# Two slots of attention scores at a time in shared PSUM banks, and rows turned by DMA instead of by TensorE

## The chip, the cores and the metric

The kernel runs on one core of a Trainium2 chip. The metric is the device time of one execution in microseconds; three runs of the kernel before gave 2230.16, 2236.23 and 2237.89, so the time before is 2236.23 (their median).

A core has five engines with queues of their own: TensorE (PE, with its weight loads shown as PEld), VectorE (DVE), ScalarE (ACT), GpSimd (POOL) and SyncE (SP, which issues nearly all DMAs here). TensorE writes to PSUM, eight banks of 512 float32 columns on each of 128 partitions; DVE and ACT read it from there.

## The reference

Four layers in a row, each added to its input after a layer norm: a Fourier mixing layer, an attention layer, and the same two again. S = 2048 rows, D = 640 columns.

```python
a = jnp.einsum("bsd,ed->bse", x, dft_hid_re)
b = jnp.einsum("bsd,ed->bse", x, dft_hid_im)
y = jnp.einsum("ts,bse->bte", dft_seq_re, a) - jnp.einsum("ts,bse->bte", dft_seq_im, b)
...
B, S, D = x.shape
H = 32; Dh = D // H; W = 256
qkv = (x @ wqkv).reshape(B, S, 3, H, Dh)   # -> q, k, v
scores = jnp.einsum("bhqd,bhkd->bhqk", q, k) * (Dh ** -0.5)
mask = (idx[:, None] - idx[None, :] >= 0) & (idx[:, None] - idx[None, :] < W)
p = _softmax(jnp.where(mask[None, None], scores, -1e9), axis=-1)
return o.transpose(0, 2, 1, 3).reshape(B, S, D) @ wo
```

The attention has 32 heads of 20 columns and looks back over a window of 256 rows.

## The kernel before, in words

Precision first: a float32 operand is split into a high and a low float16 part, and a product is three float16 products (high x high, high x low, low x high). So a projection over 640 columns is 5 x 3 = 15 matmuls into one PSUM bank.

The program is spectral(0), attention(0), spectral(1), attention(1). The attention handles 16 row tiles of 128 rows in 8 blocks of two tiles (256 rows). Its step is a *slot* g: one row tile and one pair of heads, 256 slots in all; 32 slots make a block, and four slots (both tiles, two head pairs) a *quad* n.

For each slot, in the order in which TensorE gets it:

- `scores(g)`: queries x keys, 128 rows by up to 384 keys for each of the two heads, into the tile `sp` (two banks). The keys have 62 rows in the array; the two heads lie in its two halves, at rows 0 and 64. DVE masks the diagonal block (`copy_predicated`, L1058) and takes the largest of each row (`tensor_reduce`, L1062). Every fourth slot `part_tops` splits the row maxima into float16 parts.
- `by_key(g - 7)`: the same scores keys x queries, with the row maximum as an extra row, into the tile `tp` (two other banks). ACT turns them into probabilities (L1106) in SBUF (`ptq`), and POOL clears what the mask forbids (`affine_select`, L1111 and L1113).
- For a quad: `hand_on` turns the maxima by four transposes and ACT copies them into the stacked queries (`copy_tops`, L1083, two copies); `values` multiplies probabilities by values into the bank `pv` (32 float32 matmuls) and ACT takes it to SBUF (L1139); `back` turns that by two transposes into the same bank, and DVE divides by the sum of the row (L1154, L1155).

Between these stands the *fill*: the projections of the next block (`proj_qk`, 10 units of 15 matmuls of 256 columns; `proj_v`, 4 units of 15 of 320), the output projection of finished tiles (`out_tile`, two units of 15 of 320 a tile), and in the first attention the first products of the next spectral layer (kind "next"). A planner written in Python gives the fill out in time: `run_fill(ns)` runs single matmuls until a budget is used, between 400 ns and what is due, times a factor by the slot's place in the quad (`FILL`). All instructions of TensorE are tied to this order (`issue_after`).

Row tiles must be turned (columns to partitions) before a projection: `turned` makes five transposes on TensorE for each float16 part into a bank of its own (`p3`), and ACT or DVE copies it to SBUF (L958, L956). It serves the normed rows of a block (`rows_turn`), attention outputs (`out_turn`) and rows for the next spectral layer (`next_turn`, stored to DRAM already turned and fetched by `Hidden.fetch`). These are fill units of the kind "turn".

The eight banks in an attention: `sp` two, `tp` two, `pv` one, `p3` one (turns and handing on), `pf` two in rotation (all fill).

DVE also runs the layer norms of coming rows in small pieces (`slow_step`, one a slot), behind the row maximum of the slot.

Of the kernel before, what the change touches and what calls it, by code (L numbers as in the profile page):

```python
# [34 lines left out]
FILL = (1.3, 1.12, 0.28, 1.3)  # L35
# [4 lines left out]
OUT_STEPS = (4, 2, 8)  # L40
LAST_STEPS = (1, 258)
LAST_FROM = 3
HAND_LAG = 4
KEY_LAG = 7
VALUE_LAG = 13
BACK_LAG = 15
# [4 lines left out]
NORM_STEPS = (4, 9)  # L51
# [10 lines left out]
def body(ctx: ExitStack, tc: tile.TileContext, x_in, cmat, whid, wqkv, wo, out):  # L62
# [140 lines left out]
    class Hidden:  # L203
# [18 lines left out]
        def fetch(self, s):  # L222
            load(self.xt(s).rearrange("p a b c -> p (a b c)"), self.xt_src[s])
# [121 lines left out]
    def spectral(layer, res_src, hidden, first):  # L345
        with ExitStack() as st:
# [170 lines left out]
            def main_a(r, j):  # L517
                res = [keep.tile([P, D], F32, tag="res", name="res", bufs=4) for k in range(2)]
# [173 lines left out]
            else:  # L692
                side.append(hidden.rest)
# [75 lines left out]
    def attention(layer, proj, dst, final):  # L769
        with ExitStack() as st:  # L770
# [7 lines left out]
            if layer == 0:  # L778
                ps = banks("ps")
                pv_ = banks("pv")  # L780
            else:
                pv_ = banks("pv")
                ps = banks("ps")
            p3 = banks("p3")

            def new_turn():

                return p3.tile([P, 512], F32, tag="f", name="pt") if in_turn[0] else new_f()

            in_turn[0] = True  # L790
            VS_ = {}
            pv = None
# [38 lines left out]
            def out_turn(i, k):  # L831
                if k:
                    X2[i] = keep.tile([P, D], F32, tag="res", name="x3", bufs=4)
                    load(X2[i], x2_d[i])
                else:
                    OT[i] = sb.tile([P, 2, ND, P], F16, tag="ot", name="ot", bufs=2)
                yield from turned(OS[i // 2][:, :, i % 2], k, OT[i])
                done.add((i, k))

            def last_out(i, d0, d1):  # L840

                if d0 == 0:
                    x3 = keep.tile([P, D], F32, tag="res", name="x3", bufs=4)
                    load(x3, x2_d[i])
                    OT[i] = (sb.tile([P, 2, ND, P], F16, tag="ot", name="ot", bufs=2),
                             ps.tile([P, 2, 512], F32, tag="ts"[i % 2 == 0], name="acc"), x3)
                ot, acc, x3 = OT[i]
                for k in range(2):
                    yield from turned(OS[i // 2][:, :, i % 2], k, ot, d0, d1)
                for n in range(2):  # L850
                    yield from out_products(ot, acc[:, n], n, d0, d1)
                if d1 < ND:
                    return
                for n in range(2):
                    cs = slice(n * 320, (n + 1) * 320)
                    nc.vector.scalar_tensor_tensor(x3[:, cs], acc[:, n, :320], beta, x3[:, cs], op0=OP.mult, op1=OP.add)
# [13 lines left out]
            def out_tile(i):  # L870
                ot = OT[i]
                x3 = x2 = X2.pop(i)
                for n in range(2):
# [10 lines left out]
                    if n == 0:  # L884
                        yield 136
                done.add((i, 2))
                if final:
                    load(dst[i], x3)
# [3 lines left out]
            slow, live = deque(), deque()  # L892

            def new_xs():

                while len(live) > 1:
                    for g in live.popleft():
                        for _ in g:
                            pass
                live.append([])  # L900
                return keep.tile([P, 2, D], F16, tag="xs", name="xs", bufs=2)
# [6 lines left out]
            def next_norm(i, x3):  # L908
                ys = []
                yield from norm_steps([x3], ys)  # L910
                xs = new_xs()
                split(xs[:, 0], xs[:, 1], ys[0], nc.gpsimd)
                xt = keep.tile([P, 2, ND, P], F16, tag="xto", name="xto", bufs=2)
                live[-1].extend(next_turn(i, xs, xt, k) for k in range(2))
                if i < NT - 2:
                    fill.extend(Unit(now[0] + TURN_STEPS, g, "turn", now[0], [], True) for g in live[-1])

            def split_wo():

                fs = [keep.tile([P, D], F32, tag="res", name="wst", bufs=4) for n in range(2)]  # L920
# [3 lines left out]
                for n in range(ND):  # L924
# [3 lines left out]
                    if n + 2 < ND:  # L928
                        fs.append(keep.tile([P, D], F32, tag="res", name="wst", bufs=4))
# [3 lines left out]
            def rows_norm(b, x2s):  # L933
# [3 lines left out]
                for t, y in enumerate(ys):  # L937
                    xs = new_xs()
                    split(xs[:, 0], xs[:, 1], y, nc.gpsimd)
                    live[-1].extend(rows_turn(b, xs, t, k) for k in range(2))  # L940
                    fill.extend(Unit(now[0] + ROW_STEPS, g, ("rows", b), now[0], [], True) for g in live[-1])
                    yield

            def rows_turn(b, xs, t, k):
                yield from turned(xs, k, proj.rows[b][0][:, t])
                done.add(("rows", b, t, k))

            def turned(xs, k, o, d0=0, d1=ND):
                pt = new_turn()
# [11 lines left out]
            def next_turn(i, xs, xt, k):  # L961
                yield from turned(xs, k, xt)
                if k:
                    load(xu_d[i], xt.rearrange("p a b c -> p (a b c)"))

            OS, OT, X2, done = {}, {}, {}, set()
            lastd = [0]
# [5 lines left out]
            class Unit:  # L973


                def __init__(self, at, gen, kind, due, need=(), turn=False, ns=0):
                    self.at, self.gen, self.kind, self.due, self.need, self.turn = at, gen, kind, due, need, turn
                    self.ns, self.n = ns, 0

                def ready(self):  # L980
                    return self.at <= now[0] and all(k in done for k in self.need)
# [3 lines left out]
            def next_unit(turn=None):  # L985
# [322 lines left out]
```

## Time and profile before

| | |
|---|---|
| runs | 2230.16, 2236.23, 2237.89 us |
| profiled execution | span 2233.0 us; a time of its own beside the span isn't given |
| first attention, first to last score product | about 590 to 1135 us |
| second attention, likewise | about 1685 to 2202 us |
| TensorE busy, whole span | 95% |

The page lists for each engine the busy time and its share. "Busy" of TensorE counts a pipelined matmul to its modelled end, so two matmuls that start 109 ns apart are each shown as about 273 ns long, and their overlap is counted once. The chain of waits follows the last instruction back to what released each step; a row is start, length and what ran. In groups of instructions stand count, busy time, mean ns of one, and the idle time of the engine just before them with what ended it.

### The profile page before, as it was taken

The numbers are of one execution on the slowest core, as the hardware profiler recorded it, in microseconds if no ns is written. First come the engines' busy times: TensorE is split into PE (matmuls) and PEld (weight loads), VectorE is DVE, ScalarE is ACT, GpSimd is POOL, SyncE is SP. The second block draws the span as 40 slices with busy tenths as digits, with TensorE's granted clock in tenths as the row PEclk, the third lists the DMA queues.
The fourth block names the chain that finished last, engine by engine and source line by source line (L and its number), as shares of the span: only waits on it lengthen the run. The fifth ranks groups of instructions, "written<-read, shape, count | busy, mean of one in ns | idle before, by whom it ended". The sixth has DMA issues, their size and how long they took to land.

```text
span 2233.0 us, 55112 instructions
## 1 busy us (share of the span) xinstructions
PE 2122.0 (95%) x21985; PEld 1494.7 (67%) x21985; DVE 1646.4 (74%) x3577; ACT 1288.8 (58%) x2155; POOL 1391.6 (62%) x1788
## 2 busy tenths in 40 slices
PE   7999899899999999999899999999998999999998
PEld 4767566676666766677566777777675666677765
DVE  8887958767677887887858758585767777777664
ACT  5434455443467777777754443434434777777775
POOL 5775968758355665566446858586674555566443
PEclk9999999999999999999999999999999999999999
DMA  6664646455533422333424536364743323332231
GB/s 252 219 224 143 229 138 225 156 188 175 142 79 67 103 71 73 94 91 84 134 79 160 193 127 212 110 207 145 256 133 96 83 63 85 93 87 59 57 80 37
DMA packets 187607, 292.96 MB, mean 131 GB/s; under 512 B 13908, under 2 KB 120660, under 8 KB 178004
## 3 DMA queue, kind: packets, MB, share of 16 engines
q1 hardware_dynamic: 186772, 288.77, 42.1%
q8 instruction: 172, 2.82, 0.5%
q14 instruction: 87, 0.71, 0.1%
q10 hardware_dynamic: 576, 0.66, 0.1%
HBM read 202.51 MB, written 86.87 MB: 130 GB/s over the span
## 4 chain that ended last, share of the span: by engine, by line
PE 59%; DVE 12%; DMA 4%; issue 3%; POOL 2%; ACT 2%; SPq 1%; DVEq 0%; POOLq 0%; ACTq 0%
PE pf L115 24%; PE pv L115 8%; PE y L115 7%; PE sp L115 5%; PE x L115 5%; PE z L115 5%; PE tp L115 3%; DVE m L1062 3%; DVE sp L1058 2%; PE pt L115 2%; DVE cc L489 1%; DMA res<-accd 1%; DMA x2d<-res 1%; PE acc L115 1%; DMA qs<-qkd 1%
## 5 line engine op out<-in xcount | busy, mean ns | idle before, releaser
L115 PEld LDWEIGHTS <-cc 128*128 128x128 f16 x5376 | 525.1, 98 | 215.6 <-issue 10.6
L1106 ACT ACTIVATE ptq<-tp,shift,alpha 128x768 f32<-128x768 f32 (+2 forms) x512 | 486.2, 950 | 163.6 <-PE tp L115 155.6
L115 PEld LDWEIGHTS <-big 128*128 128x128 f16 x4320 | 408.5, 98 | 151.9 <-issue 40.5
L1062 DVE TENSOR_REDUCE m<-sp 128x2 f32<-128x512 f32 (+1 forms) x512 | 345.1, 674 | 16.8
L1058 DVE COPY_PREDICATED sp<-mask,sp 128x256 f32<-128x256 int32 x448 | 190.8, 426 | 188.2 <-PE sp L115 176.5
L115 PE MATMUL pf<-early,big 128*128 128x256 f16 x2400 | 313.9, 274 | 2.9 <-ACT early L401 2.5
L1111 POOL TENSOR_SCALAR_AFFINE_SELECT ptq<-ptq 128x512 f32<-128x512 f32 x224 | 145.5, 649 | 265.4 <-ACT ptq L1106 261.7
L486 ACT ACTIVATE cc<-cs 128x512 f16<-128x512 f32 x256 | 151.6, 623 | 254.6 <-POOL cs L478 124.1
L115 PE MATMUL y<-zc,cc 128*128 128x320 f16 x1728 | 263.8, 300 | 2.4 <-DVE pf L512 2.4
L115 PE MATMUL pf<-big 128*128 128x320 f16 x1680 | 245.6, 304 | 19.2 <-DVE zc L257 9.3
L489 DVE SCALAR_TENSOR_TENSOR cc<-cs,cc 128x512 f16<-128x512 f32 x256 | 255.2, 1012 | 9.9 <-ACT cc L486 9.7
L489 DVE SCALAR_TENSOR_TENSOR cc<-cq,cc 128x512 f16<-128x512 f32 x192 | 198.7, 1036 | 0.0
L1113 POOL TENSOR_SCALAR_AFFINE_SELECT ptq<-ptq 128x512 f32<-128x512 f32 x256 | 163.9, 640 | 43.1 <-ACT ptq L1106 43.1
L115 PE MATMUL pv<-ptq,v 128*32 128x128 f32 (+1 forms) x3840 | 183.7, 330 | 0.0
L115 PE MATMUL z<-zc,cc 128*128 128x320 f16 x1152 | 178.5, 299 | 2.0 <-ACT cc L486 1.0
L115 PE MATMUL x<-zc,cc 128*128 128x320 f16 x1152 | 179.7, 299 | 0.0
L115 PE MATMUL sp<-ks,qs 62*128 62x256 f16 (+1 forms) x1792 | 153.6, 248 | 20.8 <-DVE m L1062 18.6
L115 PE MATMUL pf<-big,early 128*128 128x320 f16 x960 | 162.3, 301 | 6.4 <-DVE x L883 6.4
L1083 ACT ACTIVATE qs<-pt 2x512 f16<-2x512 f16 x224 | 131.0, 585 | 42.7 <-PE pt L115 40.0
L115 PE MATMUL tp<-qs,ks 62*128 62x128 f16 x2688 | 150.1, 217 | 3.2 <-ACT ptq L1106 2.7
L115 PE MATMUL pf<-bo,ot 128*128 128x320 f16 x840 | 147.2, 302 | 3.3 <-DVE ot L956 2.8
L167 POOL TENSOR_TENSOR xs<-lny,xs 128x640 f16<-128x640 f32 x63 | 94.2, 1497 | 83.3 <-ACT xs L166 82.6
(144 smaller groups left out, 3525.3 us busy)
## 6 DMA issues: line engine op xcount, KB each, us to landing
cq<-in_cmat_dram SPq DMA_DIRECT2D x64, 1024.0 KB
accd<-res SPq DMA_DIRECT2D x96, 320.0 KB
res<-accd SPq DMA_DIRECT2D x96, 320.0 KB
x<-x2d SPq DMA_DIRECT2D x64, 320.0 KB
qkd<-early SPq DMA_DIRECT2D x160, 128.0 KB
ks<-qkd SPq DMA_DIRECT2D x108, 160.0 KB
qs<-qkd SPq DMA_DIRECT2D x84, 160.0 KB
x2d<-res SPq DMA_DIRECT2D x32, 320.0 KB
```

Source lines behind the costliest of these rows:

```text
L115: i = getattr(nc.tensor, what)(*args, **kw)
L167: eng.tensor_tensor(lo, y, hi, op=OP.subtract)
L486: nc.scalar.activation(cc[m][:, 0], f, AF.Copy, scale=C_UP)
L489: nc.vector.scalar_tensor_tensor(cc[m][:, 1], f, C_UP, cc[m][:, 0], op0=OP.mult, op1=OP.subtract)
L1058: nc.vector.copy_predicated(sp[:, :, 2 * P:3 * P], mask[:, None, :].to_broadcast([P, 2, P]), far)
L1062: topped[0] = nc.vector.tensor_reduce(TOP[g // 4][:, g % 4], sp[:, :, c0:3 * P], axis=AX.X, op=OP.max).ins
L1083: nc.scalar.activation(o, handed[n][rs].rearrange("r (i p) t -> r i p t", i=2), AF.Copy)
L1106: nc.scalar.activation(q[:, h:h + 2, a0 + first:a0 + 3], tp[:, :, first * P:3 * P].rearrange("p a (b c) -> p a b c", c=P), AF.Sigmoid, bia ...
L1111: nc.gpsimd.affine_select(out=q[:, :, a0], in_=q[:, :, a0], pattern=[[0, 4], [-1, P]], base=0, channel_multiplier=1, compare_op=OP.is_gt, ...
L1113: ins = nc.gpsimd.affine_select(out=q[:, :, a0 + 2], in_=q[:, :, a0 + 2], pattern=[[0, 4], [1, P]], base=0, channel_multiplier=-1, compare ...
```

## The change

1. The planner's step is two slots, G = 0 to 127: both head pairs of the half quad at once. The lags are set anew in these steps.
2. Scores and keyed scores no longer have four separate banks. Two tiles of three banks (`st`, one for each half of the head pair) hold the scores of two slots in their first 768 columns and the keyed scores of two slots in the other 768. So the middle bank of each holds both. A block of the second slot that crosses a bank's edge is cut into two matmuls. DVE's and ACT's instructions keep their number and size but each takes one half (`pi`) of two slots instead of two halves of one, and in a step they are called in the order: ACT half 1, DVE half 0, DVE half 1, ACT half 0.
3. `pv` and `p3` are gone; values, back, handing on and fill share the two banks of `pf` in rotation.
4. The fill runs in whole units of 15 matmuls, one a step (a second one in even steps if there is enough budget). `hand_on` comes after the unit, at once followed by both copies.
5. Rows are turned by transposing DMAs on SP (`turn_load`), SBUF to SBUF for normed rows and attention outputs; rows for the next spectral layer are stored as they are and turned by the fetch. A turned tile counts as ready eight slots after its issue (`TURN_LAG`). Only the last two output tiles of each attention are still turned on TensorE. What was left to turn at the start of the second spectral layer (`hidden.rest`) goes away.
6. Buffers: attention outputs have three (`os`) instead of two, the four `res` buffers become two and two, and outputs are due 40 slots later.

The core of the diff:

```diff
-FILL = (1.3, 1.12, 0.28, 1.3)
+SECOND = 1500
+FULL_TO = 244
-OUT_STEPS = (4, 2, 8)
+OUT_STEPS = (4, 40, 8)
-HAND_LAG = 4
-KEY_LAG = 7
-VALUE_LAG = 13
-BACK_LAG = 15
+HAND_LAG = 1
+KEY_LAG = 3
+VALUE_LAG = 5
+BACK_LAG = 6
+TURN_LAG = 8
+UNIT = 384
...
+    def turn_load(out, in_):
+
+        with ExitStack() as order:
+            if in_turn[0] and loads:
+                order.enter_context(tc.issue_after(loads[-1]))
+            i = nc.sync.dma_start(out.rearrange("p a b c -> p (a b) c"), in_, transpose=True)
+        loads.append(i.ins)
...
         def fetch(self, s):
-            load(self.xt(s).rearrange("p a b c -> p (a b c)"), self.xt_src[s])
+            turn_load(self.xt(s), self.xt_src[s])
...
+            st = [ps.tile([P, 4 * UNIT], F32, name=f"st{k}") for k in range(2)]
+            sps, tps = ([t[:, k * 2 * UNIT:(k + 1) * 2 * UNIT].rearrange("p (e c) -> p e c", e=2) for t in st] for k in range(2))
...
-            def rows_turn(b, xs, t, k):
-                yield from turned(xs, k, proj.rows[b][0][:, t])
-                done.add(("rows", b, t, k))
+            def rows_turn(b, xs, t):
+                turn_load(proj.rows[b][0][:, t], xs.rearrange("p a b -> p (a b)"))
+                done["rows", b, t] = now[0] + TURN_LAG
...
+                for e in range(2):
...
+                        at = UNIT * e
+                        cuts = [c for c in (c0, 512 - at, c1) if c0 <= c <= c1]
+                        for d0, d1 in zip(cuts, cuts[1:]):
+                            for pi in range(2):
+                                if d1 > d0:
+                                    r = slice(64 * pi, 64 * pi + 3 * DH + 2)
+                                    matmul(st[pi][:, at + d0:at + d1], qs[r, p0 + e, t0:t0 + P],
+                                           KS[kb][r, p0 + e, k0 + d0 - c0:k0 + d1 - c0], start=True, stop=True)
...
+            def largest(G, pi):
...
+                nc.vector.copy_predicated(sp[:, :, 2 * P:3 * P], mask[:, None, :].to_broadcast([P, 2, P]), far)
+                topped[0] = nc.vector.tensor_reduce(TOP[n][:, 2 * k:2 * k + 2, pi], sp[:, :, c0:3 * P], axis=AX.X, op=OP.max).ins
...
+            def hand(n):
+                hand_on(n)
+                for pi in range(2):
+                    copy_tops(n, pi)
...
+            for G in range(NS // 2 + 1):
+                now[0] = g = 2 * G
...
+                    scores(G)
+                keyed = 0 <= G - KEY_LAG < NG // 2
+                if keyed:
+                    by_key(G - KEY_LAG)
+                if keyed:
+                    probabilities(G - KEY_LAG, 1)
+                if g < NG:
+                    for pi in range(2):
+                        largest(G, pi)
+                    if G % 2:
+                        part_tops(G // 2)
+                if keyed:
+                    probabilities(G - KEY_LAG, 0)
+                n = due(G, BACK_LAG)
+                if n is not None:
+                    back(n)
...
+                credit[0] += 2 * max(rate, 400)
+                filled = run_unit()
+                if filled and credit[0] > SECOND and G % 2 == 0:
+                    run_unit()
+                n = due(G, HAND_LAG)
+                if n is not None:
+                    if filled:
+                        hand(n)
+                    else:
+                        kept = n
```

More of the change, by code (lines that the diff above doesn't have):

```diff
@@ L50 @@
 TURN_STEPS = 8
-NORM_STEPS = (4, 9)
+NORM_STEPS = (4, 10)
 ROW_STEPS = 3
@@ L517, in main_a @@
             def main_a(r, j):
-                res = [keep.tile([P, D], F32, tag="res", name="res", bufs=4) for k in range(2)]
+                res = [keep.tile([P, D], F32, tag=f"res{j % 2}", name="res", bufs=2) for k in range(2)]
                 for k in range(2):
@@ L959, in turned @@
                 yield 56
[L961 to L967, printed above, removed]
+            OS, OT, X2, done = {}, {}, {}, {}
+            lastd, outs = [0], []
             credit = [0.0]
@@ L1022, in flush @@
             def flush(kind):
-                for u in sorted((u for u in fill if u.kind == kind and u.turn), key=lambda u: u.due):
-                    fill.remove(u)
-                    while step(u):
-                        pass
                 while any(u.kind == kind for u in fill) or (unit[0] and unit[0].kind == kind):
```

303 lines of the change are left out of this document (137 added, 166 removed).

## The prediction

> **What bounds the kernel now.** I read the page first, then a table of stretches cut at the first and last score product of each attention, then the chain of waits inside the second attention, then the engines' lists of instructions around it.
>
> ```profile
> span 2233.0 us, 55112 instructions
> PE 2122.0 (95%) x21985; PEld 1494.7 (67%) x21985; DVE 1646.4 (74%) x3577; ACT 1288.8 (58%) x2155; POOL 1391.6 (62%) x1788
> ```
> ```profile
> 590.00:1135.00 545.00, 517.92 (x6905) 360.28 (x6904) 437.30 (x1132) 406.13 (x614) 301.94 (x550) 0.99 0.34 89
> 1135.00:1176.00 41.00, 36.48 (x360) 23.03 (x356) 17.52 (x54) 19.58 (x36) 19.68 (x29) 0.96 0.30 103
> 1685.00:2202.00 517.00, 497.94 (x6721) 345.62 (x6720) 386.71 (x953) 382.92 (x575) 280.61 (x534) 1.00 0.30 73
> 2202.00:2233.00 31.00, 23.16 (x261) 14.18 (x259) 8.17 (x25) 12.48 (x20) 9.22 (x18) 1.00 0.16 54
> ```
>
> Columns: stretch, us, then busy time of PE, PEld, DVE, ACT, POOL, clock, DMA share, GB/s. The attentions (545 and 517 us, tails 41 and 31) are the only stages the change touches but for 40 turns that open the second spectral layer. TensorE is idle for 27 and 19 us of the two; it bounds them, in order. DVE is next with 80% and 75%.
>
> ```profile
> 2044.86 0.27 PE sp L115 x4
> 2045.13 0.17 PE tp L115 x6
> 2045.30 1.42 PE pf L115 x12
> 2046.72 0.22 PE pt L115 x4
> ...
> 2047.38 1.44 PE pv L115 x32
> ...
> 2050.56 0.28 PE pt L115 x5
> ...
> 2051.82 0.37 PE pv L115 x2
> 2052.19 1.64 PE pf L115 x15
> 2053.83 0.27 PE sp L115 x4
> ```
> ```profile
> 1135.76 2.04 PE pf L115 x15
> ```
>
> Chain of waits, start and length: four slots of the second attention, with nothing but TensorE on the chain; the last line is a unit of 320 columns in the first attention. One slot costs sp 0.27 + tp 0.17 and 0.10 more when the array goes back to full height (twelve pf products of 0.109 would be 1.31, not 1.42; the two transposes of pv likewise 0.27 and 0.10). In 0.27 some 0.10 is the way in: inside a slot sp takes 0.17, as in the tp line. So 0.54 a slot, 0.20 of it switching. A quad's values take 1.44, its back 0.27, its handing on 0.22, five row turns 0.28, a unit 1.64 (query, key) or 2.04 (value, output).
>
> Check on the second attention: 64 quads x (4 x 0.54 + 0.22) = 152, 60 x (1.44 + 0.27) = 103, 70 x 1.64 = 115, about 55 units x 2.04 = 113, 260 turns x 0.056 = 15, idle 19: 517, as measured. The prices hold.
>
> **The change part by part.**
>
> (1) Two slots at a time: one way in and out for two slots, 0.10 + 2 x 0.17 + 2 x 0.17 + 0.10 = 0.88, and about 0.02 for the block that is cut at a bank's edge in every other step: 0.90 instead of 1.08. 128 steps x 0.18 = 23 us a layer, **-46**.
>
> (2) Row turns off TensorE.
>
> ```profile
> L115 PE MATMUL pf<-early,big 128*128 128x256 f16 x1050 | 139.2, 273 | 0.0
> L115 PE MATMUL pt<-idh,xs 128*128 128x128 f16 x240 | 21.3, 219 | 0.0
> L115 PE MATMUL pt<-idh,os 128*128 128x128 f16 x140 | 12.4, 219 | 0.0
> L115 PE MATMUL pt<-idh,os 128*128 128x128 f16 x140 | 12.4, 219 | 0.0
> L115 PE MATMUL pt<-idh,xs 128*128 128x128 f16 x120 | 10.6, 219 | 0.0
> ```
>
> Groups of TensorE (busy, mean ns | idle): three of the first attention, two of the second. 380 + 260 turns x 0.056 (five in 0.28) = 36, and 40 of the next layer's first turns, 2: **-38**. Their PSUM copies on ACT and DVE go too; those engines were not the bound, so nothing more.
>
> (3) The old waits. The 27 and 19 us of idle belong to the old order (the largest: sp on DVE, below). I take all off, **-46**, and charge the new order's own waits.
>
> ```profile
> PE sp L115 <- DVE m L1062: 16.8, 30, 1.1
> PE sp L115 <- DVE m L1062: 11.4, 26, 0.9
> ```
>
> (4) The new chain through the banks. Scores and keyed scores of one head half lie in one three-bank tile, and the middle bank holds both. So in a step ACT takes half 1 of the keyed scores while DVE takes half 0 of the scores, and then they change over; TensorE's next scores wait for DVE's second half.
>
> ```profile
> 2196.79 0.34 PE L115 MATMUL sp<-ks,qs 62*128 62x256 f16 x4
> ...
> 2198.82 0.34 PE L115 MATMUL sp<-ks,qs 62*128 62x256 f16 x4 [0.65 <-DVE m L1062]
> ```
> ```profile
> 2191.28 1.17 ACT L1083 ACTIVATE qs<-pt 2x512 f16<-2x512 f16 x2
> ...
> 2197.34 0.99 ACT L1106 ACTIVATE ptq<-tp,shift,alpha 128x768 f32<-128x768 f32 x1 [0.52 <-PE tp L115]
> ```
> ```profile
> 2198.07 0.69 DVE L1062 TENSOR_REDUCE m<-sp 128x2 f32<-128x512 f32 x1
> ...
> 2201.32 0.43 DVE L1058 COPY_PREDICATED sp<-mask,sp 128x256 f32<-128x256 int32 x1 [0.96 <-PE sp L115]
> 2201.78 0.69 DVE L1062 TENSOR_REDUCE m<-sp 128x2 f32<-128x512 f32 x1
> ```
> ```profile
> L335 ACT ACTIVATE qf<-pf 128x256 f32<-128x256 f32 x70 | 26.5, 379 | 12.2 <-PE pf L115 9.3 <-POOL os L1157 2.6
> ```
>
> ACT starts 0.55 after a slot's first score product (2197.34 - 2196.79), so 0.89 after that of two slots. A half costs DVE 0.46 + 0.69 = 1.15, and TensorE goes on 0.06 later (2198.07 + 0.69 to 2198.82). An undisturbed step is thus at least 0.89 + 2 x 1.15 + 0.06 = 3.25.
>
> What TensorE has to do in a step: with one unit in each, a step that also makes values and hands on costs 0.90 + 1.44 + 0.22 + 1.64 to 2.04 = 4.2 to 4.6, above 3.25: no wait. The other has only 0.90 + 0.27 + 1.64 to 2.04 = 2.8 to 3.2, mean 3.0 (70 units of the one kind by the 1050 row, 56 of the other by the code: four value units for each of seven blocks, two for each of fourteen tiles). And it comes right after the handing on. ACT then still evacuates the unit before (0.38, to 0.26 into the step), makes both copies of the tops (1.17, to 1.43), only then its half 1 (0.99, to 2.45); DVE's second half ends at 2.50 + 1.15 = 3.65 and the next scores start at 3.71. After an output unit, which DVE evacuates, it is 0.18 less; mean 3.67. Stall 0.67 a short step, 61 of them with a full load in each layer: 41 us, **+82**. The two shared banks give no longer wait: the unit's bank is that of the tops, free at 1.43, and 1.43 + 1.64 or 2.04 stays under 3.7.
>
> The chain rests on ACT and DVE not being let into the middle bank together; no row of before shows it, because there sp and tp have banks of their own. Ends: none of it binds (the step is then 3.4, by the tops' bank plus the unit), or all. I take all, because the new order of calls alternates the halves. The Trainium skill ("PSUM — Partial Sum Buffer", Terms) says that two engines in one bank and quadrant at once are a collision, reads included; by it the chain is 3.7, without it 3.4, so the sum by the rule is mine and without it 33 us lower. No run here shows it yet.
>
> (5) Norm work on DVE.
>
> ```profile
> L155 DVE TENSOR_SCALAR lny<-x,lnmv,lnt 128x640 f32<-128x640 f32 x25 | 21.1, 843 | 0.0
> ```
>
> Two norm pieces a step, the largest 0.84, now follow back's 0.45 on DVE at the end of a short step; they push the long step's half 0 from 0.89 to 1.4-2.1 and the tops, which the handing on needs, by as much; that step's slack is 0.3 to 0.7. I take 0.47 a time, from none to 1.2. Twelve row norms and, in the first layer, fourteen more, at seven steps a pair or three a tile, hit 45 and 21 short steps: **+31** (0 to 79).
>
> (6) Tails. After the last scores five steps of about 3.3 us are left, then 81 products of 0.136 and some 4 us of waits for turns in the first layer: 32 for 41. In the second 26 for 31. **-13**.
>
> (7) Turning DMAs. Before has none. Nearest rows, chain of waits:
>
> ```profile
> 394.20 2.16 DMA res<-accd
> ...
> 484.53 11.13 DMA x2d<-res
> ...
> 568.31 7.76 DMA ks<-qkd
> ```
>
> Plain transfers of 320 KB took 2.2 to 11 us; 160 KB in short runs 7.8, so 15.5 for 320 KB. A turned row tile counts as ready eight slots after its issue, 8 x 517/256 = 16 us: cover for every one of these, so **0**; the price if it is gone is rival B. All go through SP in order; 26 a layer take the place of copies, not of other loads, and the 16 stores for the next layer stay. The Trainium skill ("VectorE: DVE Perf Modes", The three transpose paths) gives 1309 ns for one 128x128 turn by DMA; ten, if one after another, are 13 us by that page, an estimate that stays under the cover as well.
>
> Sum: -46 - 38 - 46 + 82 + 31 - 13 = -30; span 2203. The median of the runs is 2236.2, 3.2 above the span shown, which I keep: **2206 us**.
>
> **The rivals.**
>
> A, the short step does not stall that much (ACT takes half 1 before the tops, or the shared bank does not bind): 3.4 instead of 3.67, 0.27 x 122 = 33 less: 2173. All stalls of (4) gone would be 2124. For it: ACT is busy 74% of the second attention and could be ordered otherwise. Against: tops are ready 0.8 us before keyed scores.
>
> B, slower: a turned tile lands late. Place: the first query/key unit of a block, which TensorE takes in order with all else behind it; twelve such blocks. It decides from 30/12 = 2.5 us past the cover, 18.7 us; at 31 us, twice the row above, 12 x 15 = 180: 2386. Against it: the DMA share is 0.3.
>
> C, slower: values wait for POOL.
>
> ```profile
> L1111 POOL TENSOR_SCALAR_AFFINE_SELECT ptq<-ptq 128x512 f32<-128x512 f32 x107 | 69.1, 646 | 133.1 <-ACT ptq L1106 132.9
> ```
>
> ACT's half 0 of the short step ends at 3.44; two selects (1.3) end 1.1 into the long step, where values begin at 0.8 (first group, other blocks) and 1.7 (the masked ones). If the first group waits as well, or POOL is behind by 0.5, it is 0.4 x 122 = 49: 2255. It decides from 0.25 a pair.
>
> D, gains and new waits cancel: 2236.
>
> **How the numbers follow.** My forecast 0.45 (its own range 2185 to 2232, from the ends of (5)), A 0.20, B 0.11, C 0.14, D 0.10. A measurement here tells 0.3%, 7 us. Faster: most of the first and A, 0.58; same 0.12; slower 0.30. The range runs from between A and its bound, 2140, to C and a mild B, 2275.
>
> **What would show it.** Right: sp issued in eights and tens; idle of TensorE in the attentions 50 to 65 us each, nearly all sp waiting for DVE m, once in two steps; ACT's tops ahead of a late ptq; no pt<-os or pt<-xs; first to last sp of the second attention within 10 us of 517. (1) is wrong if TensorE's busy time does not fall by about 40 us a layer. A: idle under 30. B: pf waiting for a DMA. C: pv waiting for POOL. It would be wrong as a whole if the clock, 1.00 in the second attention, fell because of the regular gaps.

## The result

The changed kernel takes 2263.4 us (median of 4 runs, 2260.6 to 2265.2), against 2234.5 us before in the same comparison (2230.2 to 2237.9): a ratio of 1.0136, 95% interval 1.0119 to 1.0153. The change made the kernel slower by 1.4%; 2206 us and "faster" were forecast. 2263 lies inside the range given (2140 to 2275), on the side that held 0.30. The profiled execution took 2265.0 us, with a span of 2263.2 us; the ledgers below compare spans of profiled executions (2233.0 before).

First the page of the changed kernel, the same two lines as of before.

```profile
span 2263.2 us, 54344 instructions
PE 2082.2 (92%) x21529; PEld 1484.5 (66%) x21529; DVE 1655.2 (73%) x3509; ACT 1243.3 (55%) x2087; POOL 1387.2 (61%) x1788
```

TensorE's busy time fell by 40 us (2122.0 to 2082.2) and the span rose by 30: work was taken away, and more than that came back as waiting. A table of stretches of the changed kernel says where (stretch, us, then busy time of PE, PEld, DVE, ACT, POOL, clock, DMA share, GB/s). The rows are the first attention up to its last scores, its tail (what is left of it after them), and the same of the second.

```profile
593.00:1152.70 559.70, 496.28 (x6607) 350.96 (x6608) 434.14 (x1070) 380.49 (x575) 299.67 (x547) 0.98 0.43 101
1152.70:1201.00 48.30, 42.83 (x413) 28.46 (x412) 33.98 (x103) 24.50 (x46) 23.73 (x31) 1.00 0.44 139
...
1699.60:2230.40 530.80, 483.21 (x6563) 344.74 (x6564) 393.58 (x926) 364.71 (x548) 279.00 (x530) 0.99 0.39 86
2230.40:2263.20 32.80, 25.03 (x272) 15.40 (x270) 9.43 (x24) 11.93 (x20) 8.69 (x17) 0.92 0.16 51
```

From the first scores to the first product of what follows, the first attention went from 588.2 to 608.0 us and the second (to the end of the span) from 547.3 to 563.6, while the spectral layer between them went from 506.3 to 498.5. All but 2 us of the loss is in the attentions. TensorE is idle there for 63.4 + 5.5 and 47.6 + 7.8 us (loop + tail), against 27 + 5 and 19 + 8 in the kernel before. The size is about what the forecast expected (50 to 65 us an attention); the place is not. The waits of TensorE over the whole changed kernel (us in total, times, longest):

```profile
PE st L118 <- ACT ptq L1110: 24.4, 29, 3.1
PE pf L118 <- DVE tops L1069: 23.4, 28, 3.8
PE pf L118 <- ACT qs L1083: 17.0, 40, 3.7
PE pf L118 <- ACT qf L346: 12.4, 21, 0.8
...
PE st L118 <- DVE m L1062: 6.6, 34, 0.2
```

In the kernel before, the largest of them was "sp waits for DVE m". Now that one is small, and three others have come: the handing on (a transpose into `pf`) waits for the tops, a unit (`pf`) waits for ScalarE's copies of the tops (`qs`), whose bank it takes, and scores (`st`) wait for the sigmoid (`ptq`).

The chain of waits in the first attention shows a short step's end, a long step and the next one's beginning (start, length, what):

```profile
789.34 2.20 PE pf L118 x15
791.54 0.94 PE st L118 x20
...
792.54 0.44 DVE st L1061
792.98 0.02 issue
793.00 0.69 DVE m L1062
793.70 0.41 DVE st L1061
794.11 0.02 issue
794.13 0.70 DVE m L1062
794.84 0.02 issue
794.86 0.61 DVE tops L1068
795.47 0.02 issue
795.49 0.56 DVE tops L1069
796.05 0.04 issue
796.10 0.41 PE pf L118 x4
796.51 0.51 PE st L118 x6
```

The long step was forecast as TensorE's own: 4.2 to 4.6 us of work, above a chain of 3.25. Here the chain that ends it is VectorE's. After its two halves, 2.3 us with the gaps between them (792.54 to 794.84), as forecast, come the two small instructions that write the tops, `part_tops` in lines 1068 and 1069, with 0.61 + 0.56 us for 8 numbers a partition. Beside them, GpSimd's instructions at that time (start, us, engine, line, operation, operands):

```profile
794.79 0.63 POOL L1114 TENSOR_SCALAR_AFFINE_SELECT ptq<-ptq 128x512 f32<-128x512 f32 x1 [1.66 <-ACT ptq L1110]
795.38 0.63 POOL L1116 TENSOR_SCALAR_AFFINE_SELECT ptq<-ptq 128x512 f32<-128x512 f32 x1
```

The first select starts at 794.79 and the tops at 794.86; the second select starts at 795.38, the second instruction of the tops at 795.49. So the two engines' pairs run in step, and each of VectorE's ends some 0.04 us after its neighbour on GpSimd (795.47 after 795.42, 796.05 after 796.01). That is the theory the experiments start from. The groups of VectorE that hold these two lines (busy us, mean ns | idle), first of before, then of the changed kernel:

```profile
L1068 DVE TENSOR_SCALAR tops<-m 128x8 f16<-128x8 f32 x128 | 35.3, 276 | 0.2
L1069 DVE SCALAR_TENSOR_TENSOR tops<-m,tops 128x8 f16<-128x8 f32 x128 | 31.2, 244 | 0.6
```
```profile
L1069 DVE SCALAR_TENSOR_TENSOR tops<-m,tops 128x8 f16<-128x8 f32 x128 | 61.9, 484 | 4.4
L1068 DVE TENSOR_SCALAR tops<-m 128x8 f16<-128x8 f32 x128 | 50.2, 393 | 4.3
```

0.52 us a pair became 0.88. In the old order the tops were wanted a slot later, and TensorE waited for them 0.6 us in all.

### The profile page after: what moved, and what is told of

Same layout as the page of the kernel before. It is cut to its first block, busy times and chain, and to the rows that moved or that the text cites. A ratio compares the mean times of both kernels' runs of the same rounds, so it can differ in the third digit from the quotient of the medians.

```text
span 2263.2 us, 54344 instructions
## 1 busy us (share of the span) xinstructions
PE 2082.2 (92%) x21529; PEld 1484.5 (66%) x21529; DVE 1655.2 (73%) x3509; ACT 1243.3 (55%) x2087; POOL 1387.2 (61%) x1788
## 2 busy tenths in 40 slices
DMA packets 274516, 309.96 MB, mean 137 GB/s; under 512 B 102868, under 2 KB 209620, under 8 KB 264916
## 3 DMA queue, kind: packets, MB, share of 16 engines
q1 hardware_dynamic: 273684, 305.82, 46.8%
## 4 chain that ended last, share of the span: by engine, by line
PE 43%; DVE 19%; ACT 9%; issue 5%; DMA 4%; POOL 1%; SPq 1%; DVEq 0%; ACTq 0%; POOLq 0%
PE pf L118 22%; PE y L118 7%; DVE m L1062 6%; PE z L118 5%; PE x L118 4%; PE st L118 4%; ACT ptq L1110 4%; ACT qs L1083 3%; DVE st L1061 3%; DVE tops L1069 1%; DVE cc L500 1%; DVE tops L1068 1%; DVE lnt L143 1%; DVE lnst L131 1%; DMA res<-accd 1%
## 5 line engine op out<-in xcount | busy, mean ns | idle before, releaser
L1110 ACT ACTIVATE ptq<-st,shift,alpha 128x768 f32<-128x768 f32 (+2 forms) x512 | 474.2, 949 | 147.1 <-POOL ptq L1114 52.6
L1062 DVE TENSOR_REDUCE m<-st 128x2 f32<-128x512 f32 (+1 forms) x512 | 342.9, 671 | 8.8
L1061 DVE COPY_PREDICATED st<-mask,st 128x256 f32<-128x256 int32 x448 | 191.1, 427 | 184.0 <-PE st L118 145.5
L118 PE MATMUL pf<-early,big 128*128 128x256 f16 x2400 | 291.0, 274 | 18.5 <-ACT qs L1083 7.4
L1161 POOL CAST os<-o 128x160 f16<-128x160 f32 x128 | 40.5, 316 | 278.1 <-DVE o L1159 278.1
L118 PE MATMUL pf<-ptq,v 128*32 128x128 f32 (+1 forms) x3840 | 187.5, 335 | 1.4 <-POOL ptq L1116 1.4
L118 PE MATMUL st<-ks,qs 62*128 62x128 f16 (+1 forms) x2016 | 133.1, 236 | 36.2 <-ACT ptq L1110 21.7
L1083 ACT ACTIVATE qs<-pf 2x512 f16<-2x512 f16 x224 | 130.7, 583 | 56.7 <-PE pf L118 54.1
L118 PEld LDWEIGHTS pf<-ptq,v 128*32 128x32 f32 x3840 | 108.2, 111 | 59.8 <-POOL ptq L1116 4.1
L118 PEld LDWEIGHTS <-qs 62*128 62x128 f16 x2016 | 82.1, 94 | 83.1 <-issue 64.6
```

The source lines that it names most:

```text
L118: i = getattr(nc.tensor, what)(*args, **kw)
L1061: nc.vector.copy_predicated(sp[:, :, 2 * P:3 * P], mask[:, None, :].to_broadcast([P, 2, P]), far)
L1062: topped[0] = nc.vector.tensor_reduce(TOP[n][:, 2 * k:2 * k + 2, pi], sp[:, :, c0:3 * P], axis=AX.X, op=OP.max).ins
L1083: nc.scalar.activation(o, handed[n][rs].rearrange("r (i p) t -> r i p t", i=2), AF.Copy)
L1110: nc.scalar.activation(o[:, pi], tps[pi][:, :, first * P:3 * P], AF.Sigmoid, bias=shift, scale=alpha[:, 0:1])
L1161: nc.gpsimd.tensor_copy(hi, o)
```

## The experiments

The theory T: the long step is late because the tops are stretched by GpSimd's selects, which ScalarE's second sigmoid lets go just when VectorE comes to the tops. Rivals: norm work ahead of the tops (N), and the banks' chain by itself (B).

### e1: the tops before the selects

```diff
+                late = []
                 if i >= 2:
-                    nc.gpsimd.affine_select(out=q[:, :, a0], ...)
+                    late.append(nc.gpsimd.affine_select(out=q[:, :, a0], ...).ins)
                 ins = nc.gpsimd.affine_select(out=q[:, :, a0 + 2], ...).ins
+                if now[0] % 4 == 2 and now[0] < NG:
+                    for k in late + [ins]:
+                        tc.add_manual_dep(k, topped[0].name, mybir.DependencyInfo(
+                            mybir.DependencyClass.Sync, mybir.DependencyReason.DATA), reason="tops first")
```

> The changed kernel, with one order added: in the long steps (odd ones, which hand on) GpSimd's two selects wait until VectorE has written the tops (lines 1068 and 1069). Nothing is left out. Theory T: the long step, 4.91 and 4.79 us on the mean where 4.2 to 4.6 was forecast, is late because these two small instructions start at the moment at which GpSimd starts the selects, and are stretched from 0.18 + 0.17 to 0.40 + 0.52 us. T expects means below 0.22 us each, long steps of 4.4 to 4.6, TensorE's wait for tops down from 38 us to 10 or less, and 2225 to 2240 us instead of 2263. Rival N: the tops are late because of the pieces of the norms ahead of them on VectorE; then the two get short but the time falls by under 10 us. Rival B: the long step is held by the banks' chain, not by the tops: 2258 to 2264 us.

Measured: 2232.0 us (2224.2 to 2240.0), 1.0005 of before (0.9988 to 1.0022), so 31 us less than the changed kernel (29 by the two ratios, as the kernel before took 2229.9 in this comparison). The two groups in e1:

```profile
L1068 DVE TENSOR_SCALAR tops<-m 128x8 f16<-128x8 f32 x128 | 26.7, 209 | 4.3
L1069 DVE SCALAR_TENSOR_TENSOR tops<-m,tops 128x8 f16<-128x8 f32 x128 | 23.6, 184 | 4.4
```

Long steps came down from 4.91 and 4.79 us on the mean to 4.65 and 4.61 (slots 12 to 235 of each attention), short ones hardly (3.69 and 3.55 to 3.60 and 3.55, of those with one unit). The time went where T says: in these slots, the distance from the last product of a long step's unit to the first transpose of the tops adds up to 27.7 us over both attentions, where it was 52.3; that is 25 of the 30 us that the slots lost. T holds, N and B fall as explanations of these 31 us. Two expectations of T missed: the long steps stay a little above 4.4 to 4.6, and by the view of waits TensorE still waits 16.2 us for the tops (23.4 in the changed kernel), 3.7 of it at once, in the first steps.

### e2: no selects but the last step's

```diff
-                if pi:
+                if pi or G < NG // 2 - 1:
                     return
```

> The changed kernel without GpSimd's selects behind the sigmoid, but for the last slot's (the causal window's edges are not cut, so this part of the computation is left out); GpSimd keeps its casts, splits and norms. T expects what the order of e1 gives and a little more, as nothing of the selects is left to collide with anything: 2218 to 2238 us, tops below 0.22 us each. N and B expect 2255 to 2264. If GpSimd slows VectorE in general, the reductions (0.69) and predicated copies (0.43) get shorter as well; T alone expects them unchanged within 3%, as they read PSUM.

Measured: 2222.7 us (one run). The tops took 191 and 186 ns. The reductions (688 ns in the second attention in both) and the predicated copies that read PSUM (427 and 426) did not change. So the selects do not slow VectorE in general. Order alone (e1) recovers 31 of the 41 us that leaving the selects out does.

### e3: the turning DMAs alone, in the old order

The kernel before, with parts 5 and 6 of the change: `turn_load`, the queue of late turns, the three buffers of `OS`, the split `res` and the later due time of outputs; scores, banks and lags as before. Its core:

```diff
-                yield from turned(OS[i // 2][:, :, i % 2], k, OT[i])
-                done.add((i, k))
+                turn_load(OT[i], OS[i // 2][:, i % 2].rearrange("p a b -> p (a b)"))
...
-                yield from turned(xs, k, proj.rows[b][0][:, t])
+                turn_load(proj.rows[b][0][:, t], xs.rearrange("p a b -> p (a b)"))
...
-            load(self.xt(s).rearrange("p a b c -> p (a b c)"), self.xt_src[s])
+            turn_load(self.xt(s), self.xt_src[s])
...
-                if g % 4 in (2, 3) or g >= NG + HAND_LAG:
-                    run_fill(ns / 2)
-                    turn_unit()
-                    run_fill(ns / 2)
-                else:
-                    run_fill(ns)
+                run_fill(ns)
```

> The kernel before with one part of the change alone: rows are turned by transposing DMAs (row norms, outputs, next layer's rows), and scores are made a slot at a time in their old banks and old order. If the turns are worth what TensorE spent on them: 38 us in the attentions, and the 10.6 us by which the second spectral layer fell in the changed kernel: 2234 - 49 = 2185 us (2178 to 2196). Rival: the old order has other limits (VectorE busy 80% and 75% of the attentions) and gives half of it back as waits of scores for VectorE's m: 2200 to 2215. Rival: the transposing DMAs cost what they save: 2225 to 2240.

Measured: 2187.5 us (2186.1 to 2191.4), 0.9806 of before (0.9780 to 0.9832), as expected. This is the fastest of the study. Its stretches, cut as above:

```profile
593.00:1109.00 516.00, 494.18 (x6514) 337.09 (x6513) 418.96 (x1081) 382.56 (x575) 301.02 (x546) 0.99 0.47 111
1109.00:1157.50 48.50, 44.32 (x401) 28.05 (x396) 28.30 (x89) 24.93 (x47) 22.79 (x31) 0.93 0.33 107
...
1657.80:2152.00 494.20, 479.88 (x6433) 328.19 (x6432) 377.98 (x924) 366.84 (x548) 278.49 (x528) 1.00 0.41 93
2152.00:2187.00 35.00, 26.80 (x289) 16.34 (x286) 9.37 (x27) 12.39 (x20) 9.22 (x18) 0.99 0.17 57
```

From the first scores to the last it takes 516 and 494 us, against 545 and 517 before and 560 and 531 in the changed kernel, with TensorE idle for 22 and 14 us. So the change is a gain of 46 us of span (2233.0 to 2187.0) and a loss of 76 (2187.0 to 2263.2). The whole loss belongs to the rest of the change: two slots at a time with what goes with it, the shared banks, the whole units and the new lags. No run makes one of these without the others.

### e4 and e6: both engines in the same tile

In e4 the two sigmoids of a step change places:

```diff
-                    probabilities(G - KEY_LAG, 1)
+                    probabilities(G - KEY_LAG, 0)
...
-                    probabilities(G - KEY_LAG, 0)
+                    probabilities(G - KEY_LAG, 1)
```

> The changed kernel with the two sigmoids of a step in the other order (half 0 first), so that ScalarE and VectorE want the same three-bank tile at the same time. Nothing is left out. Forecast part (4): the shared middle bank lets only one of them in, so a step becomes 0.95 (first scores to the keyed scores' end) + 0.99 + 2 x 1.15 + 0.99 = 5.2 us at least, against 3.25 to 3.47 (short) and 4.3 to 5.0 (long): 1.8 + 0.4 us more a pair of steps, and up to 3 with what stands behind it, 128 pairs: 270 to 380 us more, 2530 to 2640 us. If the bank does not serialise them, the time stays within 15 us of 2263.

Measured: 2255.0 us (one run). But this settles nothing: VectorE's order is planned, and the plan had mirrored it too. The trace shows that the two engines still kept out of each other's way: in one step ScalarE's first sigmoid starts at 787.72 and VectorE's first half beside it, at 787.69. e6 writes VectorE's order out as well:

```diff
-                    for pi in range(2):
-                        largest(G, pi)
+                    largest(G, 0)
+                    with tc.issue_after(topped[0]):
+                        largest(G, 1)
```

> As e4, with VectorE's order written out as well (half 0, then half 1): in e4 VectorE had been planned in the mirrored order, half 1 first, and so its 2255 us say nothing on the bank. Now ScalarE and VectorE want the same three-bank tile at the same time. If the shared middle bank lets only one in: a step of 0.95 + 0.99 + 2 x 1.15 = 4.25 us at least before the next scores' half 1, short ones 4.3 and more against 3.6 on the mean, long ones with the tops 5.2 to 5.6 against 4.9: 128 x 0.7 + 128 x 0.4 = 140 us more, 2380 to 2430. If the bank does not serialise them: 2248 to 2268.

Measured: 2585.5 us (one run), 322 more than the changed kernel, where 140 were forecast. The largest wait of VectorE in e6, and that of TensorE:

```profile
DVE st L1061 <- ACT ptq L1110: 383.0, 242, 3.6
```
```profile
PE st L118 <- ACT ptq L1110: 228.5, 132, 2.5
```

And one step, ScalarE's and then VectorE's list:

```profile
899.84 0.99 ACT L1110 ACTIVATE ptq<-st,shift,alpha 128x768 f32<-128x768 f32 x1 [0.95 <-DVE m L1062]
...
901.70 0.99 ACT L1110 ACTIVATE ptq<-st,shift,alpha 128x768 f32<-128x768 f32 x1 [0.60 <-PE st L118]
...
904.98 0.99 ACT L1110 ACTIVATE ptq<-st,shift,alpha 128x768 f32<-128x768 f32 x1 [1.39 <-DVE m L1062]
```
```profile
902.73 0.43 DVE L1061 COPY_PREDICATED st<-mask,st 128x256 f32<-128x256 int32 x1 [1.00 <-ACT ptq L1110]
```

VectorE's first half starts when ScalarE's first sigmoid is done (901.70 + 0.99), and ScalarE's second waits for VectorE's last reduction. So the shared middle bank does serialise the two engines, as part (4) took it, and the alternation of halves is what makes the order bearable. It does so by waits in the program; what the chip would do without them was not tried. The Trainium skill ("PSUM — Partial Sum Buffer", Terms) calls two engines in one bank and quadrant at once a collision, an error; in e6 no two were let in, which agrees with the page but does not show its error.

The 140 us were short because that sum ends with VectorE's halves. TensorE's next scores also wait for the second sigmoid, which comes behind them and which e4's expectation had counted: a step of 5.2 us, and 2530 to 2640 us in all, in which 2585.5 lies. From one second sigmoid to the next it is 5.14 here (899.84 to 904.98). The granted clock of the two attentions was 0.93 and 0.92 in e6, against 0.98 and 0.99 in the changed kernel; no run shows what that adds.

### e5: handing on one step later

```diff
-HAND_LAG = 1
-KEY_LAG = 3
-VALUE_LAG = 5
-BACK_LAG = 6
+HAND_LAG = 2
+KEY_LAG = 4
+VALUE_LAG = 7
+BACK_LAG = 8
```

> The changed kernel with the handing on one step later: it follows the short step's unit instead of the long step's, and keyed scores, values and back follow one and two steps later (the four lags become 2, 4, 7 and 8). Selects are where the change put them. Theory H: both waits that e1 shows or leaves, TensorE for the tops (38 us in the changed kernel) and the short step's unit for the bank of the tops (42 us), come from handing on directly behind the tops; with a short step between, the tops have 3 us to be written, contention or not, and their copies are ScalarE's first work in the long step, whose unit comes 2.4 us after its start. H expects long steps of 4.2 to 4.5, short ones of 3.3 to 3.6, a pair 0.7 less than now: 2 x 60 x 0.7 = 84 us less, some 7 us a layer back for a longer tail: 2185 to 2200. Rival T (only the stretched tops count): as e1, 2225 to 2240. Rival B (the chain through the banks sets both steps): copies ahead of the keyed scores make the long step longer, 2245 to 2275.

Measured: 2213.4 us (2212.0 to 2216.0), 0.9916 of before (0.9901 to 0.9931), 50 us less than the changed kernel, with the selects left where they collide, but 13 above H's range. Of the steps with one unit, the long ones take 4.24 and 4.13 us, about as expected, and the short ones 3.90 and 3.69, which is 0.1 to 0.6 above the expectation. Two places of its chain of waits say why. In a stretch of the first attention without norm work the chain is all TensorE:

```profile
766.92 0.78 PE st L118 x22
767.70 2.63 PE pf L118 x21
770.32 0.78 PE st L118 x20
771.11 3.58 PE pf L118 x47
```

A short step takes 3.40 us here (766.92 to 770.32) and the long one behind it 4.37 (to 774.69), with no wait in them. Where the pieces of a norm run, VectorE is the chain:

```profile
682.19 0.06 DVE lnt L140
...
683.92 0.10 issue
684.01 0.42 DVE st L1061
...
685.49 0.23 DVE o L1159
```

Eight small instructions of a norm (lines 140 to 144) had started at 682.10, behind the long step's tops. The short step's scores begin at 681.72, so VectorE's first half was due some 0.95 later; it starts at 684.01, and `o`, whose bank the handing on needs, ends at 685.72. So H holds for the long step and for the tops; in the short step the norm's delay comes in its place.

### e7 and e8: where the norms' pieces go

e7 is e1 with four pieces in each long step and none in the short ones; e8 is e5 with two in the short steps and one in the long.

```diff
-                for _ in range(2):
+                for _ in range(2 if g >= NG else 4 * (G % 2)):
                     slow_step()
```
```diff
-                for _ in range(2):
+                for _ in range(2 if g >= NG else 1 if G % 2 else 2):
                     slow_step()
```

> e1 with the pieces of the norms four in each long step, behind the tops, in place of two in every step. After e1 TensorE still waits 13.8 and 6.5 us for the tops in the two attentions. Theory N2 (forecast part (5)): these are the norm pieces of the short steps, which push the long step's half 0: the waits fall to 5 us together and the time to 2215 to 2222. Rival: four pieces behind the tops push the short step's half 0 instead, and its chain, which has no slack, pays: 2230 to 2245.

> e5 (handing on one step later) with one piece of the norms in each long step in place of two; the short steps keep two. In e5 long steps came down to 4.24 and 4.13 us as meant, but the short ones rose to 3.90 and 3.69, with 24 us of TensorE waiting ahead of the handing on for VectorE's division (o), whose bank the tops are turned into. Theory N (forecast part (5), in its new place): pieces issued behind the long step's tops push the short step's VectorE work; with half as many the wait falls from 24 to 12 us or less: 2213 less 10 to 15 us, 2198 to 2204. Rival: the short step is full without them (its chain of banks), so 2210 to 2216.

Measured: e7 2231.6 us (0.9990 of before, 0.9977 to 1.0003), the same as e1: its rival holds. Long steps fell by 0.1 (to 4.53 and 4.53), and short ones rose to 3.83 and 3.60. e8 2238.7 us (1.0027 of before, 1.0014 to 1.0041), 25 more than e5, where 10 to 15 less was expected. The wait for `o` did fall (22.2 to 8.5 us), but the first attention took 606.3 us in place of 581.9: twenty of its short steps took two units in place of six, and over the whole kernel scores wait 20.6 us for the transfers of queries (`qs`), where it was 4.4. That the slower norms deliver their rows later, and so make the units late, is argued; the granted clock of that attention, 0.94 against 0.98, may have a part too. The second attention, with half the norm work, took 540.5 in place of 541.1. None of the places tried for these pieces gained time.

### e9: one unit a step, always

e1 without the second unit of some short steps:

```diff
-                if filled and credit[0] > SECOND and G % 2 == 0:
-                    run_unit()
```

> e1 without the second unit that some short steps take (line 1291 of the changed kernel and the one under it); block ends still make good what is due. Ten short steps so took two units, and after slot 118 eleven steps had none, in which TensorE waits for the banks' chain. Theory F (the forecast's even spread of one unit a step does not hold, and each unit that is taken twice and missed later costs up to 1.5 us): 10 x 1.0 to 1.5 less, 2217 to 2223. Rival: units that are due at a block's end then come in a lump there, so 2228 to 2240.

Measured: 2293.2 us (1.0264 of before, 1.0244 to 1.0284), 61 us above e1. Both expectations missed. The largest wait of TensorE in e9 (2.5 us in e1):

```profile
PE st L118 <- DMA qs<-qkd: 45.8, 12, 9.8
```

Queries of the next block are then made so late that their way through memory ends after the block's first scores are due. So the double units are no mistake of the plan; the blocks' due times ask for them.

## Why the prediction was wrong, step by step

Two sums carry this section: of TensorE's start-to-start distances in the two attentions, the part that the same pair of instructions needs where nothing waits (its work) and the rest (its waits), worked out from the traces' instructions. They run from the first scores to the first product of what follows, in the second attention to its last product. Where the line is drawn between the two is a choice that moves the waits of all five kernels by tens of us; the differences between kernels move by a few.

| us, both attentions | before | e3 | changed | e1 | e5 |
|---|---|---|---|---|---|
| work | 540.5 + 512.3 | 524.4 + 498.4 | 501.9 + 477.2 | 501.4 + 477.3 | 501.9 + 476.6 |
| waits | 47.7 + 30.9 | 40.1 + 26.6 | 106.1 + 82.6 | 83.1 + 70.7 | 80.0 + 60.5 |
| span | 2233.0 | 2187.0 | 2263.2 | 2229.5 | 2214.3 |

**(1), -46, right.** From e3 to the changed kernel the work falls by 22.5 + 21.2 = 44 us. The busy time does not show it (PE 2081.8 in e3's page, 2082.2 in the changed kernel's), so the test that the prediction set for it, 40 us of busy time a layer, was a bad one: in the chain above, fifteen products that start 0.136 apart are shown as 2.20 us busy, since the last one counts with its modelled 0.30 us, and a wait of up to 0.16 behind it shows as busy.

**(2) and (7), -38 and 0, right.** e3 gives 46 of span. 30 is work (16.1 + 13.9), where 36 were forecast, 12 are waits (that they went with the turns' copies is argued), 6 come from the spectral layer (506.3 to 500.2), where 2 were forecast, less 2 in what stands ahead. No wait of TensorE for a turned row stands in either kernel's list, so rival B did not come. The times to landing of these transfers are not in the profile:

```profile
ot<-os SPq DMA_TRANSPOSE x28
early<-xs SPq DMA_TRANSPOSE x24
big<-xud SPq DMA_TRANSPOSE x16
```

So the 16 us of cover are shown to be enough only in so far as nobody waited. The packets under 512 B rose from 13908 to 102868, and the spectral layer did not suffer.

**(3), (4) and (5), the step that failed.** Together with the tails they were summed to -46 + 82 + 31 - 13 = +54; from the kernel before to the changed one the waits rose by 58.4 + 51.7 = 110 (by 122 from e3, which has 12 fewer). The failed sentence is that of the long step in (4): "4.2 to 4.6, above 3.25: no wait". It left out that the handing on, in the same step, needs the tops, which come after both halves on VectorE: in the chain above they end 4.5 us into the step (791.54 to 796.05). Part (5) even names the tops as what the handing on needs, but prices only what norms add ahead of them; the tops' own price was never set in. At the 0.18 us each that they take alone it would by the forecast's terms have done no harm: 3.25 + 0.36 is still before the handing on, which comes 4.0 to 4.4 into the step. But beside GpSimd's selects the price was 0.88 on the mean, and 1.17 in the chain above, where VectorE also starts 1.0 us into the step instead of 0.89; and long steps took 4.91 and 4.79 us in place of 4.38.

In slots 12 to 235 the two attentions take 488.4 + 475.7 = 964 us; 56 pairs of 3.67 + 4.38 each, with the share of (5), would be 2 x 451 + 27 = 929. Of these 35 us e1 takes away 30 (469.3 + 464.7 = 934). That the rest is only 5 us is in part luck: in e1 long steps still take 4.65 and 4.61 us, which the 27 us charged for norms about cover, and five short steps of each attention take two units, which the others, with 3.60 and 3.55, mostly make up for.

The chain through the banks was read rightly (e6; undisturbed steps of 3.24 and 3.25 us in the trace). The short step's size was right too, 3.67 forecast and 3.69 and 3.55 measured with one unit, but not its place. TensorE waits little for `m` ahead of the scores (6.6 us). It waits ahead of the unit, for ScalarE's copies of the tops that hold the unit's bank: from back's last transpose to the unit's first product it takes 27.0 us in the slots above, in either attention, where e5, which hands on later, takes 15.6 and 12.3. The forecast had said that this bank gives no longer wait.

**(6), -13, wrong.** The tails take 48.3 and 32.8 us where 32 and 26 were forecast, 23 more. e3's tails are 48.5 and 35.0: making two slots at a time does not shorten a tail, as output products and not scores fill it. The nine steps ahead of the last scores take 46.8 and 36.2 where 5 x 3.67 + 4 x 4.38 = 36 each were due, 11 more: three of them in the first attention and five in the second have no unit ready, and last 3.2 to 4.8 us all the same, with VectorE's and ScalarE's work in the chain; their units fall into other steps, one of which takes 11.3 us, with 3.7 of wait for the copies of the tops. The prediction counted one unit in every step. That is read from the trace only; e9, which changes where units go, changes more than this.

**Rivals.** A: the stall of the short step stayed. C: values wait 1.4 us for GpSimd in all, so 49 was far off; GpSimd's selects did cost, but on VectorE. D did not come. The slower outcome (0.30) was held by mechanisms other than the one that brought it, so that the range holds 2263 is luck.

**What would show it.** The idle time of 50 to 65 us an attention nearly came true (69 and 55, tails included), but not as scores waiting for `m` once in two steps. The granted clock of the second attention went from 1.00 to 0.99, some 5 us of 531 by these figures (an estimate), so it did not make the loss. First to last scores of the second attention were to stay within 10 us of 517; they took 531.

## What to carry to other kernels

When a change moves a small instruction from a place with slack onto the path between two steps, price it as the trace shows it at its worst, with the neighbour that will run beside it then, and not by its shortest length. A resource that two engines share in turn (here a bank) can be planned by alternation, but every step then has a floor of that chain, which the steps without other work pay in full. And of a change in several parts, run each part alone: here one half was worth 2% and the other cost 3.5%.

## What the runs showed of the hardware

GpSimd stretches some of VectorE's instructions, and only some. Instructions of the changed kernel, by whether a GpSimd instruction ran during more than 0.02 us of them (mean ns, count in brackets, worked out from the trace; in the `neg` row a few long ones make the mean, its median is 444):

| VectorE, line | operands in SBUF | alone | beside GpSimd |
|---|---|---|---|
| tops, 1068 (one input, 128x8) | all | 177 (4) | 400 (124) |
| tops, 1069 (two inputs, 128x8) | all | 182 (12) | 515 (116) |
| lny, 158 (one input, 128x640) | all | 602 (11) | 893 (29) |
| cc, 500 (two inputs, 128x512) | all | 681 (60) | 1110 (196) |
| predicated copy from `neg`, 1061 | two inputs | 429 (40) | 580 (24) |
| predicated copy from `st`, 1061 | one input, rest PSUM | 427 (246) | 425 (202) |
| reduction m, 1062 | input PSUM | 690 (127) | 686 (353) |
| bn_stats, 131 (one input, 128x320) | all | 479 (14) | 479 (82) |
| lnt, 143 (128x1) | all | 267 (56) | 271 (136) |

The price does not show as idle time before the instruction but as its own length, so no list of waits names GpSimd. Where it ends is sharp: in the changed kernel 77 instructions of line 1068 and 115 of line 1069 took over 0.22 us, and every one of them ends 0.03 to 0.04 us after the end of a GpSimd instruction. So these lasted until their neighbour was done, however short they are alone. Overlap by itself is not enough: 47 more of line 1068 overlapped a GpSimd instruction and took no longer than 0.22 us.

The Trainium skill ("SBUF — State Buffer", Who interferes with whom) says that a VectorE instruction with two SBUF inputs, or one in a mode that takes both of the engine's ports, contends with GpSimd for a pair of ports, and that the one that comes second waits; one with at most one SBUF input, outside such a mode, doesn't. The table agrees as far as it goes, and e1 and e2 agree in time; which mode the one-input instructions ran in, no run here shows. The prediction had not weighed this rule, though the kernel before had its trace: means of 276 and 244 ns, against some 0.18 us alone.
